# A fused attention and feed-forward kernel: the last attention block cut into one half and two quarters of its queries, one tanh moved to the end, two inverse deviations moved to GpSimd, new thresholds in the static schedule

## The chip, the cores and the metric

The kernel runs on one core of a Trainium2 chip. The metric is the device time of one execution in microseconds (us). The span, which the profile shows, starts with the first instruction and ends with the last; it is 1.8 to 2.1 us shorter than that time in most executions. Some executions show a stretch of half clock of TensorE, about 3.4 us long; they are called dipped below, and dipped and undipped ones are told apart throughout. Four of the fourteen profiles show such a dip; the other executions are sorted by their spans and mean clocks alone, so that for them it is a judgement.

The engines are named as in the profile: PE is TensorE, ACT is ScalarE, DVE is VectorE, POOL is GpSimd.

## The reference

```python
# x [1, 2048, 448] bf16; H = 16 heads of 28; F = 1792
xn = layernorm(x)
q, k, v = split_heads(xn @ wqkv)
p = softmax(q @ k.T / sqrt(28))
s = merge_heads(p @ v) @ wo
g = silu(gelu(xn @ w1 + b1) @ w2 + b2)
return x + s * g
```

## The kernel before

The scores are 16 blocks (4 groups of 4 heads, by 4 chunks of 512 queries), each of 64 tiles of 128 keys by 512 columns: 1024 tiles. PE writes score tiles into a ring of banks, ACT takes two or three tiles at a time through one exp instruction into the P buffers, PE multiplies P by the values. Some tiles are taken from ACT: DVE copies the scores out as integers ("eviction") and works out the exponential with four more operations and a scaling. Which tiles, is decided when the program is built: the code simulates its own schedule with a duration for each task, and a threshold for each block says how much backlog DVE may have (THS) and how near to the end of a block (SLACKS) a tile may still be taken.

```python
LATE_GAP, LATE_SUB = 3, 14
THS = (8.0, 4.0, 7.0, 6.0, 4.0, 6.0, 9.0, 6.0, 3.0, 3.0, 8.0, 8.0, 8.0, 3.0, 6.0, 8.0)
SLACKS = (6.0, 5.0, 6.5, 5.0, 9.0, 6.5, 9.0, 6.0, 3.0, 4.0, 6.0, 6.0, 8.0, 6.0, 8.0, 6.0)
SEM = 0.07                       # modelled handover between tasks
# ... cut: pick_late(u), whether unit u gives its last tile to DVE
        n = 64 if sub < NBLK - 1 else 16
        r = m % n
        if len(ms) < 3 or not K.late_on or sub == 0 or r < 4 or GU - 1 <= u <= GU + 1:
            return False
        left = (n - 1 - r) / 3.0 * 1.364 + SLACKS[m // 64]
        # ... cut: second tile of an open pair
            bl = K.backlog()
            one = max(bl, 4.1) + 7.2 > left
            if not K.ys or bl > THS[m // 64] or bl + 4.8 > left or sub > LATE_SUB:
                return False
```

The last block is worked as four quarters of 128 queries, so that little is left to do after the last exp; a score tile of a quarter holds four pieces of 128 columns.

```python
    def pieces(self, m):                        # block 15
        s, r = r // 16, r % 16
        return b, r % 4, [(4 * (r // 4) + k, 128 * s, 128, 128 * k) for k in range(4)], r == 15, s

    def p_epi4(self, s):                        # end of quarter s, cut to its operations
        # DVE tensor_copy(E, acc)                          cast
        # PE  matmul(bank, selb, E)                        sums of the four heads
        # DVE reciprocal(R, bank)
        # DVE tensor_tensor(dst, E, R, mult)               product
        # then: PE matmuls with wo (output), DVE multiply by the gate g, DVE add of x, DMA
```

The inverse deviation of the layernorm (rstd) of each chunk is a logarithm and an exponential on ACT, and the gate of each chunk is a tanh on ACT followed by four DVE operations:

```python
        yield _Task(ACT, lambda eng: eng.activation(K.lnv[:, sl], K.mv[:, sl, 1], ACTF.Ln, bias=K.epsc[:, 0:1]), ...)
        yield _Task(ACT, lambda eng: eng.activation(K.rstd[:, sl], K.lnv[:, sl], ACTF.Exp, scale=-0.5), ...)
        # ... cut
        yield _Task(ACT, lambda eng: eng.activation(sg, fb, ACTF.Tanh, scale=0.5), ...)     # 4 x 448 columns
```

The softmax here doesn't subtract the row's maximum and nothing guards it: scores larger than these inputs give would overflow.

## Time and profile before

| | before |
|---|---|
| time, three runs | 486.66 us (486.65 to 486.67) |
| span of the profiled execution | 484.67 us |
| first exp starts | 12.61 us |
| last exp ends | 478.45 us |
| tail after it | 6.22 us |
| busy: PE, ACT, DVE, POOL | 438.8, 471.8, 389.7, 34.5 us |
| tiles on DVE | 70 of 1024 |

I read such a kernel as three terms: the head up to the first exp, the stream of exps on ACT, and the tail. The prediction shows the lines for it. (Texts written earlier took tails from spans rounded to 0.1 us: 6.25 before. The figures here are worked out from unrounded times.) One more number is used below, the excess of waits. From the end of one exp to the end of the next, in long stretches without a wait, it is 1.343 us for three tiles and 0.917 us for two. What a step between two neighbouring exps takes beyond that is summed up as excess: 1.15 us for the kernel before.

### The profile page before, as it was taken

To read this page: it belongs to the slowest core of one execution; us is meant where nothing else is said; L and a number is where in the kernel's file an instruction comes from. 1 tells how busy PE (TensorE), PEld (TensorE's weight loads), DVE (VectorE), ACT (ScalarE), POOL (GpSimd) and SP (SyncE) were. 2 spreads that over 40 slices of the span, in tenths; PEclk is the share of its full clock that TensorE was granted. 3 is DMA by queue.
4 is the path that set the end of the run, shared out by engine and by line. 5 is a ranking of instruction groups with operands and counts; after the bars stand their busy time and mean duration, and the time that the engine had idled before them with its cause. 6 is when DMAs were issued, how large, how long until landed. Compare 5 with 4: busy or idle time off the path is not lost.

```text
span 484.7 us, 10440 instructions
## 1 busy us (share of the span) xinstructions
PE 438.8 (91%) x4393; PEld 170.2 (35%) x4428; DVE 389.7 (80%) x562; ACT 471.8 (97%) x393; POOL 34.5 (7%) x71
## 2 busy tenths in 40 slices
PE   6998989998899998899899989989999999989895
PEld 4443333332232323333323442233333333434553
DVE  8946789988769989979877968798887888878354
ACT  5999999999999999999999999999999999999994
POOL 7260000000001000000001000010100100010000
PEclk9999999999999999999999999999999999999998
DMA  8401000000000000000400000000010010201010
GB/s 252 143 8 29 1 0 1 1 2 3 0 1 1 1 1 1 1 3 0 134 1 0 1 2 0 1 2 8 31 39 1 2 39 1 64 13 41 1 62 20
DMA packets 8289, 11.11 MB, mean 23 GB/s; under 512 B 1649, under 2 KB 6897, under 8 KB 8242
## 3 DMA queue, kind: packets, MB, share of 16 engines
q1 hardware_dynamic: 8098, 10.21, 6.9%
q8 instruction: 35, 0.57, 0.5%
q10 hardware_dynamic: 144, 0.23, 0.1%
q14 instruction: 12, 0.10, 0.1%
HBM read 8.61 MB, written 1.84 MB: 22 GB/s over the span
## 4 chain that ended last, share of the span: by engine, by line
ACT 45%; PE 34%; issue 16%; DVE 3%; POOL 0%; ACTq 0%; DVEq 0%
ACT P L1136 43%; PE ring L1105 9%; PE acc L1322 5%; PE misc L1053 5%; PE ring L995 4%; PE acc L845 2%; PE misc L683 2%; PE misc L995 1%; PE misc L1411 1%; PE acc L827 1%; ACT h L1032 1%; ACT w L1067 1%; PE ring L937 1%; PE misc L1394 0%; PE misc L1246 0%
## 5 line engine op out<-in xcount | busy, mean ns | idle before, releaser
L1136 ACT ACTIVATE P<-ring 128x1536 bf16<-128x1536 f32 (+1 forms) x350 | 431.3, 1482 | 0.7 <-PE ring L1105 0.4
L1105 PE MATMUL ring<-qT,kT 32*128 32x512 bf16 (+1 forms) x1208 | 136.4, 349 | 29.7 <-ACT P L1136 23.5
L1322 PE MATMUL acc<-P,vaug 128*32 128x512 bf16 (+1 forms) x1146 | 94.8, 351 | 1.2 <-DVE E_sb L1372 0.5
L1105 PEld LDWEIGHTS ring<-qT,kT 32*128 32x128 bf16 x1208 | 36.6, 91 | 140.2 <-ACT P L1136 130.3
L1159 DVE TENSOR_SCALAR x_sb<-ring 128x512 int32<-128x512 f32 x62 | 42.6, 688 | 20.8 <-PE ring L1105 20.2
L1053 PE MATMUL misc<-w,h 128*128 128x448 bf16 x224 | 51.9, 355 | 0.1
L845 PE MATMUL acc<-ident,zero 128*128 128x128 bf16 x546 | 47.0, 221 | 0.6 <-DVE E_sb L1372 0.4
L1322 PEld LDWEIGHTS acc<-P,vaug 128*32 128x32 bf16 x1146 | 25.1, 94 | 49.9 <-issue 45.0
L845 PEld LDWEIGHTS acc<-ident,zero 128*128 128x128 bf16 x546 | 31.6, 98 | 20.7 <-issue 16.9
L995 PE MATMUL misc<-xnT,w 128*128 128x512 bf16 x125 | 35.2, 382 | 1.9 <-issue 1.4
L1384 POOL CAST rhi<-rc 128x16 bf16<-128x16 f32 x15 | 7.8, 521 | 403.7 <-DVE rc L1382 304.4
L978 DVE CAST h<-misc 128x512 bf16<-128x512 f32 x35 | 24.1, 687 | 9.8 <-PE misc L995 9.6
L1053 PEld LDWEIGHTS misc<-w,h 128*128 128x128 bf16 x224 | 17.5, 97 | 23.2 <-issue 11.3
L1276 DVE SCALAR_TENSOR_TENSOR kT<-kT 128x1024 f32<-128x1024 f32 (+1 forms) x20 | 23.3, 1167 | 0.3
L1278 DVE SCALAR_TENSOR_TENSOR kT<-kT 128x1024 f32<-128x1024 f32 (+1 forms) x20 | 23.3, 1167 | 0.3
L1280 DVE SCALAR_TENSOR_TENSOR x_sb<-x_sb,kT 128x1024 uint16<-128x1024 int32 (+1 forms) x20 | 23.3, 1164 | 0.4
L1274 DVE SCALAR_TENSOR_TENSOR kT<-kT 128x1024 f32<-128x1024 f32 (+1 forms) x20 | 23.3, 1163 | 0.4
L995 PE MATMUL ring<-xnT,w 128*128 128x512 bf16 x81 | 19.5, 380 | 0.9 <-ACT h L1032 0.7
L1274 DVE SCALAR_TENSOR_TENSOR w<-w 128x1024 f32<-128x1024 f32 (+1 forms) x17 | 19.7, 1159 | 0.3
L1278 DVE SCALAR_TENSOR_TENSOR w<-w 128x1024 f32<-128x1024 f32 (+1 forms) x17 | 19.7, 1157 | 0.3
L1280 DVE SCALAR_TENSOR_TENSOR x_sb<-x_sb,w 128x1024 uint16<-128x1024 int32 (+1 forms) x17 | 19.7, 1156 | 0.2
L1276 DVE SCALAR_TENSOR_TENSOR w<-w 128x1024 f32<-128x1024 f32 (+1 forms) x17 | 19.6, 1154 | 0.1
(142 smaller groups left out, 439.1 us busy)
## 6 DMA issues: line engine op xcount, KB each, us to landing
h<-in_A_x_dram SPq DMA_DIRECT2D x4, 448.0 KB, 3.3
w<-in_B_w_dram SPq DMA_DIRECT2D x1, 1568.0 KB, 7.3
x_sb<-in_A_x_dram SPq DMA_DIRECT2D x3, 448.0 KB, 5.5
w<-in_B_w_dram SPq DMA_DIRECT2D x1, 1344.0 KB, 8.2
out_dram<-h SPq DMA_DIRECT2D x6, 224.0 KB, 2.0
h<-in_A_wqkv_dram SPq DMA_DIRECT2D x3, 168.0 KB, 5.5
out_dram<-h SPq DMA_DIRECT2D x4, 112.0 KB, 1.7
wo<-in_A_wo_dram SPq DMA_DIRECT2D x16, 24.5 KB
```

Of the source, the lines that this page charges most:

```text
L845: ins = eng.matmul(K.acc[:, 0:128], K.zero[:, :], K.ident[:, :], start=False, stop=True, skip_group_check=True)
L978: yield _Task(DVE, lambda eng: eng.tensor_copy(dst, bank), [tok], wr, 0.69, 0.0, 2)
L995: ins = eng.matmul(bank, K.w1[:, kt, ft * 128:(ft + 1) * 128], K.xnT[:, kt, c * 512:(c + 1) * 512], start=(kt == 0), stop=(kt == KT - 1))
L1053: ins = eng.matmul(ps, hv[:, ft, t * 128:(t + 1) * 128], K.w2[:, ft, :], start=(ft == 0), stop=(ft == FT - 1))
L1105: return eng.matmul(K.ring[:, RB[m], col:col + nq], K.kT[32 * j:32 * j + 32, g, t * 128:(t + 1) * 128], K.qT[32 * j:32 * j + 32, g, c * 51 ...
L1136: return eng.activation(K.P[:, p0:p0 + n, :], K.ring[:, b0:b0 + n, :], ACTF.Exp, scale=SM_SCALE)
L1159: yield _Task(DVE, lambda eng, m=m, i=i, half=half: eng.tensor_scalar(K.ysb[i][:, 512 * half:512 * half + 512], K.ring[:, RB[m], :], SM_SC ...
L1274: yield _Task(DVE, lambda eng: eng.scalar_tensor_tensor(u, v, EXP_A, v, op0=ALU.add, op1=ALU.mult), [tv], [tu], d1, 0.0, 4)
L1276: yield _Task(DVE, lambda eng: eng.scalar_tensor_tensor(u, u, EXP_B, u, op0=ALU.add, op1=ALU.mult), [tu], [tu], d1, 0.0, 4)
L1278: yield _Task(DVE, lambda eng: eng.scalar_tensor_tensor(u, v, EXP_D, u, op0=ALU.mult, op1=ALU.add), [tv, tu], [tu], d1, 0.0, 4)
L1280: yield _Task(DVE, lambda eng: eng.scalar_tensor_tensor(pl.bitcast(dt.uint16), y, 2.0 ** -9, u, op0=ALU.mult, op1=ALU.add), ty + [tu], [K. ...
L1322: return eng.matmul(K.acc[32 * j:32 * j + 32, q0:q0 + nq], K.vaug[:, t, 4 * g + j, :], ap[:, col:col + nq], tile_position=(0, 32 * j), sta ...
```

## The change

Its intent is to take work out of the ACT stream: four small ACT instructions to GpSimd, a quarter of one tanh to the end, and more tiles to DVE, also in the last block, whose first half is now worked as one piece long enough to have such tiles. The half has 32 tiles of two pieces of 256 columns; two quarters follow. Repeated and mechanical parts are cut.

```diff
-LATE_GAP, LATE_SUB = 3, 14
-THS = (8.0, 4.0, 7.0, 6.0, 4.0, 6.0, 9.0, 6.0, 3.0, 3.0, 8.0, 8.0, 8.0, 3.0, 6.0, 8.0)
-SLACKS = (6.0, 5.0, 6.5, 5.0, 9.0, 6.5, 9.0, 6.0, 3.0, 4.0, 6.0, 6.0, 8.0, 6.0, 8.0, 6.0)
+LATE_GAP, LATE_SUB = 3, 15
+THS = (8.0, 4.0, 7.0, 8.0, 4.0, 7.0, 9.0, 6.0, 6.0, 8.0, 8.0, 8.0, 8.0, 8.0, 7.0, 3.0)
+SLACKS = (6.0, 5.0, 3.0, 5.0, 2.0, 6.5, 9.0, 6.5, 3.0, 4.0, 7.0, 6.0, 8.0, 6.0, 8.0, 3.0)
-SEM = 0.07
+SEM, OWN = 0.07, 0.03
@@ start_of
+        own = self.evsem[t.E]
-            s = max(s, b.tw + SEM)
+            s = max(s, b.tw + (OWN if b.w is not None and b.w[0] is own else SEM))
@@ p_ln2, chunks 2 and 3
+            yield _Task(POOL, lambda eng: eng.tensor_scalar(K.lnv[:, sl], K.mv[:, sl, 1], LN_EPS, None, op0=ALU.add), ...)
+            yield _Task(POOL, lambda eng: eng.tensor_tensor(K.rstd[:, sl], K.lnv[:, sl],
+                                                            K.mhalf[:, 0:1].to_broadcast([128, len(ts)]), ALU.pow), ...)
@@ p_silu, last chunk
-        yield _Task(ACT, lambda eng: eng.activation(sg, fb, ACTF.Tanh, scale=0.5), ...)
+        nt = 4 if c < C - 1 else 3
+        yield _Task(ACT, lambda eng: eng.activation(sg[:, 0:nt, :], fb[:, 0:nt, :], ACTF.Tanh, scale=0.5), ...)
+        if nt < 4:
+            yield ("until", lambda: K.exp_m == MTOT - 1)
+            # tanh of the fourth tile on ACT, then on POOL: o = tanh * fb; o = o + fb
@@ pieces, last block
-        s, r = r // 16, r % 16
-        return b, r % 4, [(4 * (r // 4) + k, 128 * s, 128, 128 * k) for k in range(4)], r == 15, s
+        if r < 32:
+            return b, r % 4, [(2 * (r // 4) + k, 0, 256, 256 * k) for k in range(2)], r == 31, 0
+        s, r = r // 16 - 1, r % 16
+        return b, r % 4, [(4 * (r // 4) + k, 128 * (s + 1), 128, 128 * k) for k in range(4)], r == 15, s
@@ pick_late
-        n = 64 if sub < NBLK - 1 else 16
+        n = 64 if sub < NBLK - 1 else 32
@@ p_epi4: ts = ((0, 1), (2,), (3,))[s]; one cast for the piece, then sums, reciprocal and product for each tile
```

## The prediction

> **What bounds the kernel now.** I read the page first: the busy totals, then the slices over time.
>
> ```profile
> PE 438.8 (91%) x4393; PEld 170.2 (35%) x4428; DVE 389.7 (80%) x562; ACT 471.8 (97%) x393; POOL 34.5 (7%) x71
> ...
> DVE  8946789988769989979877968798887888878354
> ACT  5999999999999999999999999999999999999994
> ```
>
> ScalarE (ACT) is full in every slice but the first and the last. VectorE (DVE) has holes, most of them in the last three slices (3, 5, 4 tenths). Next the busy time by stretches:
>
> ```profile
> core 0: us, PE busy (x) PEld busy (x) DVE busy (x) ACT busy (x) POOL busy (x), PEclk, DMA share, GB/s
> ...
> 233.00:260.00 27.00, 24.34 (x226) 8.29 (x229) 20.53 (x27) 27.00 (x23) 0.41 (x2) 1.00 0.19 59
> ...
> 287.00:314.00 27.00, 25.18 (x199) 8.75 (x198) 19.88 (x26) 26.97 (x22) 0.00 (x0) 1.00 0.01 2
> ...
> 435.00:449.00 14.00, 13.09 (x145) 6.06 (x143) 11.34 (x15) 14.00 (x12) 0.00 (x0) 1.00 0.10 35
> 449.00:462.00 13.00, 11.58 (x279) 6.35 (x277) 5.11 (x11) 13.00 (x11) 0.41 (x2) 1.00 0.06 19
> 462.00:478.50 16.50, 15.80 (x368) 9.38 (x365) 8.17 (x16) 16.45 (x13) 0.00 (x0) 1.00 0.12 38
> 478.50:484.70 6.20, 1.00 (x18) 0.45 (x18) 2.56 (x5) 0.00 (x0) 0.00 (x0) 0.80 0.06 21
> ```
>
> ACT is busy 27.0 of 27.0 us in stretch after stretch; it stops at about 478.5. So the span is three terms: a head to the first exp (12.6 us in the timeline), an ACT stream without gaps from 12.6 to 478.45 (465.85 us), and a tail of 6.25 us with no ACT work. Anything taken out of the stream shortens the kernel by its own length, unless it makes ACT wait. DVE works only 5.1 of 13 us from 449 to 462, where the last block starts: that is the hole the change aims at.
>
> What one ACT step costs comes from the groups by form:
>
> ```profile
> L1136 ACT ACTIVATE P<-ring 128x1536 bf16<-128x1536 f32 x255 | 356.7, 1615 | 0.0
> L1136 ACT ACTIVATE P<-ring 128x1024 bf16<-128x1024 f32 x94 | 101.9, 1126 | 0.7 <-PE ring L1105 0.4
> ```
>
> The durations overlap from one instruction to the next, so they are not steps. Steps come from start to start: the score matmuls that follow each three-tile exp start at 461.89 and, eleven steps on, at 476.67, so 1.344 us a step. Two-tile steps: seven exps in a row from 18.94, the last ending at 25.48, so starting 1.1 before; (24.4 - 18.94)/6 = 0.91 us. One tile of 512 columns moved from ACT to DVE is worth 1.344 - 0.91 = 0.43 us. Today 70 tiles of 1024 are on DVE: 62 evictions of ring tiles plus 8 around the gelu stage. The 94 two-tile exps agree: 32 at the start, 62 robbed of a tile. No eviction starts after 434.9, because the last block is forbidden to have any.
>
> **What the Trainium skill says.** "Perfetto Trace Analysis", section Identifying the Most-Contended Engine, says to take occupancy for ScalarE and work on that engine first; with 97% the trace agrees. "ScalarE: Activation LUTs", section What ACT_TABLE_LOAD costs, gives 0.833 ns per element in a lane and some 93 ns of overlap between neighbours: 512 columns would be 0.427 us, and the 0.43 from the steps agrees. The section on table sets of that page puts tanh in the exp set, so moving a tanh behind the exps should cost no table load; the three loads in the trace (1.283 us each) are at the start and around gelu, none at the tanhs. "GPSIMD Engine Reference", section Elementwise, gives about 2.6 cycles per element for an operation with two inputs (0.97 us for 448 elements at its 1.2 GHz, an estimate from that page). The trace has one of this size, the 128x448 square at 1.033 us, and I use that.
>
> **The change, part by part.**
>
> 1. Rstd of chunks 2 and 3. Removed from ACT: two logarithm-and-exponential pairs. At 18.48 the logarithm starts and at 18.94 the next big exp: 0.46 us. The second pair runs from 25.33 to 25.81: 0.48. Sum 0.94 us out of the stream. Added on GpSimd: an add and a power on four columns. A four-column operation there took 0.229 us; the power is in no trace, and the 1.1 us that the code's own schedule gives it is all I have. So rstd comes about 0.23 + 1.1 + 0.2 of handovers = 1.5 us after the statistics (17.89), at 19.4 instead of 19.03. That is 0.4 us later, while ACT comes to use the keys 0.5 to 0.9 earlier. This matters for chunk 2: its keys are written from 26.95 to 27.69, and the scores of the seventeenth two-tile unit start at 27.93, so they follow almost at once. The ring of scores gives ACT only some 0.3 us of reserve there. Of the 0.94 us I therefore expect 0.55 to stay (estimate: sometimes the delay is absorbed, since the transposes of that chunk start 1.5 us after their inputs; sometimes all but 0.3 is lost to a wait for keys).
>
> 2. The last tanh. One tanh on 1792 columns takes 408.92 to 410.51 on ACT, 1.59 us of stream. With 1344 columns it should be 1.59 - 448 x 0.833 ns = 1.22. Saved: 0.37 us. The fourth part runs behind the last exp, where ACT is idle. It then needs two GpSimd operations: 0.47 (tanh) + 2 x 1.03 + 3 handovers of 0.07 = 2.74 us after the last exp. The tail today takes from 478.45 to 481.48, 3.03 us, before the multiply by this gate: last matmuls, copy 0.29, sum matmul, reciprocal 0.96, product 0.29, output matmul. So it fits with about 0.3 us to spare, and the tail stays at 6.25, or grows by a few tenths if GpSimd is slowed by VectorE beside it. One VectorE operation of 0.62 us falls away as well.
>
> 3. The last block as a half and two quarters. Keys and queries are the same; score tiles of the half are two pieces of 256 columns, not four of 128, so PE gets fewer instructions, and the last quarter, which sets the tail, is untouched. What counts is that the half may use VectorE exps. It has 32 tiles, about 32/3 x 1.344 = 14.3 us of ACT. A pair of tiles on VectorE is two evictions of 0.69, one scaling of 0.69 and four operations of 1.22: 6.95 us. VectorE has 7.9 us free from 449 to 462. One pair fits, perhaps a pair and a single: 2 to 4 tiles, I take 3. Saved: 3 x 0.43 = 1.3 us. The end of the half waits for these exps, but two quarters of 7.2 us each follow in which that can be made up, and the P buffers (21 tiles, seven units) cover 9 us.
>
> 4. The new thresholds and the own-engine handover of 0.03. They change no instruction's cost, only how many tiles the static schedule gives to VectorE and in which order. VectorE is idle 6.5 us in 233 to 260 and 7.1 in 287 to 314; just there the thresholds go up most (3 to 6, 3 to 8), also later (3 to 8), while two early blocks get a stricter end. Over the fourteen stretches of 27 us from 44 to 422 the idle time is about 57 us. If 11 of it become exps at 3.5 us a tile, that is 3 tiles, 1.3 us. This number is a choice: I can see the room but not what the schedule does with it. From -1 to +8 tiles is possible.
>
> Sum: 0.55 + 0.37 + 1.3 + 1.3 = 3.5 us. 486.66 - 3.5 = 483.1.
>
> **The rivals.**
>
> A. VectorE becomes the bound. It is at 80% over the span, 25.1 of 27 in the fullest stretches. If the higher thresholds overfill it, evictions release their ring tiles late, the scores wait and then ACT. Against it: the same rule already bounds the backlog, and ACT shows no such wait today. It would leave the gain at 0.5 to 1.5 us: 485 to 486.
>
> B. The keys of chunk 2 come late and ACT waits about 1 us near 27 us. For it: the tight timing of step 1. Against it: the slack ahead of the transposes. It would cost 0.4 more than my sum: 483.5.
>
> C. The GpSimd products end after the output matmul, and the tail grows by 0.3 to 0.8 us: at worst 483.9.
>
> D. The re-tuning fills VectorE's idle time better than I think, with ten more tiles in all than I count: 4 us more, 479. For it: 57 us of idle. Against it: much of it is pieces under 2 us between operations that wait for PE.
>
> **Range and chances.** A, B and C together could take about 2 us from the gain, D could add 2 or 3 in the plausible case. So 480.5 to 485.3 for 8 in 10. Faster by over 2% means below 476.9, which needs 9.7 us, or some 19 more tiles on VectorE beside the rest (66 us of its time); 2% chance. Slower by over 2% would need a new stall of 10 us: 1%. The rest is within 2%.
>
> **What would show it.** Right: ACT still without gaps from 13 to the end of its exps; no logarithm at 18 or 25 us; one tanh of 1344 columns, one of 448 after the last exp; about 76 VectorE tiles (two to four of them after 445 us); a tail of 6.2 us from the last exp. Wrong in step 1: an ACT wait on PE near 27 us, or a power far from 1.1 us. Wrong in step 2: the last multiply waits for GpSimd, not PE. Wrong in 3 or 4: a tile count outside 71 to 80, or new ACT waits at block ends. The most doubtful term is 4.

## More of the kernel before

The tail of the kernel before, from its timeline (start us, duration us, engine, line, operation, output and input):

```profile
478.60 0.41 PE L1322 MATMUL acc<-P,vaug 128*32 128x128 bf16 x16 [0.35 <-ACT P L1136]
479.05 0.29 DVE L1354 CAST E_sb<-acc 128x128 bf16<-128x128 f32 x1 [2.71 <-PE acc L1322]
...
479.40 0.23 PE L1357 MATMUL ring<-E_sb,selb 128*128 128x128 bf16 x1 [0.40 <-DVE E_sb L1354]
479.67 0.96 DVE L1360 RECIPROCAL w<-ring 128x128 f32<-128x128 f32 x1 [0.32 <-PE ring L1357]
```

The attention matmuls start 0.15 us after the last exp, the sum matmul 0.35 us after the start of the cast. The chain is free of other work.

## The result, and the profile after

| | before | changed |
|---|---|---|
| median of six executions | 486.75 us (486.65 to 487.69) | 483.99 us (483.74 to 485.26) |
| undipped executions | | 483.74 to 483.99 (four) |
| dipped executions | | 484.90 and 485.26 (two) |
| ratio of means | | 0.9945 (0.9931 to 0.9959) |

A ratio here is the mean time of one kernel's runs over that of the other's in the same rounds, so it is not quite the ratio of the medians. The class "within 2%" was right, and 483.99 lies in the range, 0.9 above the predicted 483.1. The gain of medians is 2.8 us, where 3.5 was forecast. The output is correct.

The changed kernel's page, the lines that stand against those of before:

```profile
PE 438.5 (91%) x4232; PEld 168.1 (35%) x4268; DVE 407.6 (84%) x592; ACT 468.8 (97%) x390; POOL 43.2 (9%) x77
...
DVE  8946888989978989989878749899997999889785
ACT  5999999999999999999999999999999999999994
```

ACT lost 3.0 us of busy time, DVE gained 17.9, and ACT is still full. The stretches at the end, by busy time of each engine:

```profile
core 0: us, PE busy (x) PEld busy (x) DVE busy (x) ACT busy (x) POOL busy (x), PEclk, DMA share, GB/s
...
449.00:462.00 13.00, 12.11 (x220) 6.21 (x218) 10.26 (x19) 13.00 (x11) 0.95 (x2) 1.00 0.01 3
462.00:476.50 14.50, 13.70 (x300) 8.10 (x300) 9.99 (x19) 14.50 (x13) 0.00 (x0) 1.00 0.12 42
476.50:483.10 6.60, 1.89 (x24) 0.73 (x22) 3.86 (x8) 0.42 (x1) 2.06 (x2) 0.77 0.16 52
```

DVE now works 10.26 of 13 us from 449 to 462 (5.11 before): the hole was used. The last stretch is 6.6 us long, not 6.2. The groups by form on ACT (the mean is in ns, after the busy time):

```profile
L1160 ACT ACTIVATE P<-ring 128x1536 bf16<-128x1536 f32 x249 | 349.3, 1606 | 1.0 <-PE ring L1129 1.0
L1160 ACT ACTIVATE P<-ring 128x1024 bf16<-128x1024 f32 x100 | 108.2, 1133 | 0.7 <-PE ring L1129 0.6
...
L1080 ACT ACTIVATE w<-w 128x1344 bf16<-128x1344 bf16 x1 | 1.4, 1423 | 0.0
```

255 three-tile exps became 249 and 94 two-tile ones became 100: six tiles more are on DVE, 76 in all, and one tanh has 1344 columns. On GpSimd the power is there, two of them:

```profile
L645 POOL TENSOR_TENSOR rstd<-lnv,mhalf 128x4 f32<-128x4 f32 x2 | 2.1, 1035 | 0.2
```

**The dip.** The profiled execution was a dipped one (484.90). By stretches of the length of the dip:

```profile
39.80:43.20 3.40, 3.07 (x35) 1.16 (x31) 2.27 (x6) 3.40 (x4) 0.00 (x0) 1.00 0.17 38
43.20:46.60 3.40, 3.36 (x14) 0.59 (x14) 1.38 (x2) 2.65 (x3) 0.00 (x0) 0.50 0.00 0
46.60:50.00 3.40, 3.02 (x29) 1.06 (x27) 2.62 (x6) 3.16 (x3) 0.02 (x1) 1.00 0.00 0
```

and the second of these stretches in an undipped execution of the same kernel (the next run):

```profile
43.20:46.60 3.40, 3.13 (x22) 1.00 (x23) 2.20 (x5) 3.40 (x4) 0.00 (x0) 1.00 0.00 0
```

For 3.4 us the granted clock is 0.50, PE executes 14 matmuls where the undipped execution has 22, and ACT has work for only 2.65 us of 3.40. The Trainium skill, page "TensorE: Matmul & The Clock Gate", section "Part 1: The HAM clock gate (the "warmup" mystery)", says that the clock is either half or full, and judged over a free-running window of about 3.4 us; this trace agrees, with 0.50 and 3.4 us. The kernel before with new thresholds alone, profiled below, shows the same dip, from 44.1 to 47.5 us, and before itself has executions with spans of 485.6 to 486.3 us beside those of 484.7 to 485.4. So a dip is no effect of the change, and I compare undipped executions from here on. What sets it off stays open.

### The profile page after: what moved, and what is told of

The parts are those of the page before. It is cut to its first block, busy times and chain, and to the rows that moved or that the text cites. A ratio compares the mean times of both kernels' runs of the same rounds, so it can differ in the third digit from the quotient of the medians.

```text
span 483.1 us, 10155 instructions
## 1 busy us (share of the span) xinstructions
PE 438.5 (91%) x4232; PEld 168.1 (35%) x4268; DVE 407.6 (84%) x592; ACT 468.8 (97%) x390; POOL 43.2 (9%) x77
## 4 chain that ended last, share of the span: by engine, by line
ACT 45%; PE 32%; issue 17%; DVE 5%; ACTq 0%; DVEq 0%
ACT P L1160 42%; PE ring L1129 9%; PE acc L1346 6%; PE misc L1065 4%; PE acc L857 3%; PE misc L695 2%; ACT h L1044 2%; PE misc L1007 1%; PE acc L839 1%; PE misc L949 1%; PE misc L1442 1%; PE ring L1007 1%; ACT w L1080 1%; PE ring L949 1%; DVE kT L1298 0%
## 5 line engine op out<-in xcount | busy, mean ns | idle before, releaser
L1129 PE MATMUL ring<-qT,kT 32*128 32x512 bf16 (+2 forms) x1144 | 136.5, 360 | 26.1 <-ACT P L1160 22.0
L1346 PE MATMUL acc<-P,vaug 128*32 128x512 bf16 (+2 forms) x1074 | 95.0, 363 | 1.0 <-issue 0.5
L1183 DVE TENSOR_SCALAR x_sb<-ring 128x512 int32<-128x512 f32 x68 | 46.8, 688 | 14.2 <-PE ring L1129 13.0
L1415 POOL CAST rhi<-rc 128x16 bf16<-128x16 f32 x15 | 10.3, 686 | 402.5 <-DVE rc L1413 255.6
L857 PE MATMUL acc<-ident,zero 128*128 128x128 bf16 x516 | 44.8, 221 | 0.0
L857 PEld LDWEIGHTS acc<-ident,zero 128*128 128x128 bf16 x516 | 29.8, 98 | 21.3 <-issue 19.4
L1304 DVE SCALAR_TENSOR_TENSOR x_sb<-x_sb,kT 128x1024 uint16<-128x1024 int32 (+1 forms) x24 | 26.7, 1111 | 0.5
L1302 DVE SCALAR_TENSOR_TENSOR kT<-kT 128x1024 f32<-128x1024 f32 (+1 forms) x24 | 26.6, 1110 | 0.5
L1298 DVE SCALAR_TENSOR_TENSOR kT<-kT 128x1024 f32<-128x1024 f32 (+1 forms) x24 | 26.5, 1104 | 0.6
L1300 DVE SCALAR_TENSOR_TENSOR kT<-kT 128x1024 f32<-128x1024 f32 (+1 forms) x24 | 26.4, 1102 | 0.2
L1298 DVE SCALAR_TENSOR_TENSOR w<-w 128x1024 f32<-128x1024 f32 (+1 forms) x18 | 20.3, 1128 | 0.3
L1300 DVE SCALAR_TENSOR_TENSOR w<-w 128x1024 f32<-128x1024 f32 (+1 forms) x18 | 20.3, 1130 | 0.2
L1302 DVE SCALAR_TENSOR_TENSOR w<-w 128x1024 f32<-128x1024 f32 (+1 forms) x18 | 20.3, 1129 | 0.1
```

The costliest lines, as they stand in the source:

```text
L857: ins = eng.matmul(K.acc[:, 0:128], K.zero[:, :], K.ident[:, :], start=False, stop=True, skip_group_check=True)
L1129: return eng.matmul(K.ring[:, RB[m], col:col + nq], K.kT[32 * j:32 * j + 32, g, t * 128:(t + 1) * 128], K.qT[32 * j:32 * j + 32, g, c * 51 ...
L1183: yield _Task(DVE, lambda eng, m=m, i=i, half=half: eng.tensor_scalar(K.ysb[i][:, 512 * half:512 * half + 512], K.ring[:, RB[m], :], SM_SC ...
L1298: yield _Task(DVE, lambda eng: eng.scalar_tensor_tensor(u, v, EXP_A, v, op0=ALU.add, op1=ALU.mult), [tv], [tu], d1, 0.0, 4)
L1300: yield _Task(DVE, lambda eng: eng.scalar_tensor_tensor(u, u, EXP_B, u, op0=ALU.add, op1=ALU.mult), [tu], [tu], d1, 0.0, 4)
L1302: yield _Task(DVE, lambda eng: eng.scalar_tensor_tensor(u, v, EXP_D, u, op0=ALU.mult, op1=ALU.add), [tv, tu], [tu], d1, 0.0, 4)
```

## The experiments

**The changed kernel again.** No edit: the same kernel. Its five executions were all undipped.

> The changed kernel, unaltered. Two levels are expected, because the six first runs had two: about 483.9 us where the granted TensorE clock is 1.0 over the whole span, about 485.0 where it is 0.993 (the profiled run had the clock at 0.50 from 44 to 46 us and ACT waiting 0.96 us for scores at 46.84). Theory: the dip alone is the 1.2 us between the levels, and a trace without it has ACT waits of only 0.6 us after the first exp. Rival: the levels are something else, and a trace at clock 1.0 still shows that wait.

Measured: 483.73 us (483.72 to 483.90), before 486.67 to 487.34 undipped; ratio 0.9922 (0.9908 to 0.9937). The span is 481.93. Its waits of ACT for score tiles, with total, number and longest, first in the dipped profile and then here:

```profile
ACT P L1160 <- PE ring L1129: 1.5, 3, 1.0
```

```profile
ACT P L1160 <- PE ring L1129: 0.5, 2, 0.3
```

The dip cost 1.15 us of span (483.08 against 481.93), 1.0 of it in that one wait. With the dip gone, the balance between the two profiled executions can be made, all in us. "Other ACT work" is the length by which it widens the step between two exps.

| term | before | changed | difference |
|---|---|---|---|
| start of the first exp | 12.61 | 13.20 | +0.59 |
| six tiles at 0.426 | | | -2.56 |
| rstd of chunks 2 and 3 (2 x 0.41) | 0.82 | 0 | -0.82 |
| rstd of chunk 1, now ahead of the first exp | 0.41 | 0 | -0.41 |
| last tanh | 1.58 | 1.20 | -0.38 |
| excess of waits | 1.15 | 1.62 | +0.47 |
| stream (sum of the last five, 0.02 unexplained) | 465.84 | 462.12 | -3.72 |
| tail | 6.22 | 6.61 | +0.39 |
| span | 484.67 | 481.93 | -2.74 |

The stream lost 3.72 us, but 0.41 of that is the pair of chunk 1, which the prediction did not have and which only stands in the head now; without it the stream lost 3.31 of the predicted 3.5. Head and tail gave back 0.57 beside that pair. The longer tail and the terms of the stream are what the next runs take apart.

A profile's head has some chance in it. The matmuls of the first transposes start 107 ns apart until the trace's first record of a full clock, and 55 ns apart from there on. That record lies anywhere between 6.3 and 9.7 us in the fourteen profiles: at 7.76 before, 8.66 here. The first input statistics also start 0.16 us later here than before (3.87 against 3.71).

**Pinned tiles.** A change in one part moves the static schedule, and with it which tiles go to DVE. For some runs I therefore gave `pick_late` a list of tiles in place of its thresholds. With the changed kernel's own list it builds the changed kernel's program again (checked by building both: they differ in line numbers alone).

```diff
+PIN = [(m, h, m == p[-1]) for p in PAIRS for h, m in enumerate(p)]
@@ pick_late
-            if not K.ys or bl > THS[m // 64] or bl + 4.8 > left or sub > LATE_SUB:
+        if not PIN or PIN[0][0] > m ...:
```

**The two tiles of the half given back to ACT.** The list without tiles 974 and 980. Theory: each is worth 0.43, and the DVE exps of the half also disturb the tail. Rival: the tail has another cause.

> The changed kernel with the two VectorE tiles of the last block's half given back to ACT; all other 74 tiles fixed as in the changed kernel. Theory: ACT pays 2 x 0.43 = 0.86 us more, but the half ends without waiting for VectorE's chain (465.2 us now), so the third output of the last chunk is out before the last exp and the tail falls from 6.65 back to about 6.25: net +0.4 to +0.5, about 484.4. Rival: the tail's extra 0.4 has another cause (the moved gate, the single free bank), it stays, and the kernel is +0.86: 484.8.

Measured: 484.60 to 484.67 us undipped (two dipped, 486.08 and 486.09); ratio 0.9950 (0.9934 to 0.9965). The stream is 462.97, so 0.85 longer, which is 2 x 0.426; excess 1.62 as in the changed kernel. The tail is 6.61, as there: it did not recover. The half is worth its two tiles and no more, and the longer tail does not come from DVE exps in it; here the rival held.

**All six tiles given back.** The list of the kernel before, 70 tiles, on the changed kernel.

> The changed kernel with exactly the 70 VectorE tiles of the kernel before. Theory: every tile is worth 0.43 us of ACT, six are 2.6 us, less 0.4 that the tail gains back: +2.2, about 486.1. Rival: the four tiles outside the last block were won only by overfilling VectorE, part of them comes back as waits, and their loss costs less than 0.25 us each: 484.9 to 485.3.

Measured: 486.96 to 486.99 undipped (two dipped, 487.61); ratio 0.9993 (0.9979 to 1.0007). The stream is 465.49: 2.52 longer than with 74 tiles. Four tiles are 1.70 of it; the other 0.80 is excess (2.42 against 1.62). That list was made for another schedule, which may be why; this run does not show it. Without its six tiles the changed kernel is level with before, so the rest of the change brings about as much as its longer tail and this misfit cost; a clean value of the tiles cannot be read from it.

**Rstd back on ACT, tiles pinned.**

```diff
@@ p_ln2
-        if c < 2:
+        if c < 4:
```

> The changed kernel with rstd of chunks 2 and 3 on ACT again, the same number of VectorE tiles in each block. Theory: the two pairs cost ACT 0.94 us, less the 0.30 us wait at 28.3 us that the changed kernel has there: +0.6, about 484.5. Rival 1: the late keys ate the whole gain: 483.9, no difference. Rival 2: the wait at 28.3 has nothing to do with rstd: +0.94, 484.8.

Measured: 488.41 us (488.38 to 488.73); ratio 1.0019 (1.0006 to 1.0032). That is 4.7 us more than the changed kernel. The waits of ACT show why this run measures something else:

```profile
ACT P L1162 <- PE acc L1339: 2.6, 2, 1.7
```

ACT waits 2.6 us for P buffers (the attention matmuls that release them), at two places around 403 and 405 us; the changed kernel waits for no P buffer. The likely reason, not tested, is that the pinned tiles don't fit the schedule that comes of the shifted start. As a whole the run is confounded, but not at its beginning: the first 32 exps are block 0, which gives no tile to DVE in any of these kernels. From the start of the first exp to the end of the 32nd, less the 0.41 of chunk 1's pair where it lies inside, the traces give:

| first 32 exps | us |
|---|---|
| before | 30.85 |
| changed | 30.35 |
| changed, rstd back on ACT (this run) | 31.23 |
| before, rstd on GpSimd alone (next run) | 30.85 |
| changed, own-engine handover of 0.07 (below) | 30.85 |

So in the changed order rstd on GpSimd is worth 0.88 us here, and the change as a whole 0.50.

**Rstd on GpSimd alone, in the kernel before.** Only `p_ln2` as in the change; 70 tiles, the same as before. Theory: of the 0.8 to 0.9 us some half stays. Rival: the keys come late and eat it.

> The kernel before with rstd of chunks 2 and 3 on GpSimd alone; the schedule keeps the same 70 tiles in each block. Theory: two pairs of 0.47 us leave ACT, and ACT waits some 0.3 us more near 28 us: -0.6 us against the kernel before. Rival 1: late keys eat all of it: 0. Rival 2: no wait at all: -0.94.

Measured: 486.73 to 487.06 undipped (one dipped, 487.73), before 486.58 to 487.09 undipped; ratio 0.9996 (0.9982 to 1.0009). The stream is 465.84, to the hundredth that of before: 0.82 of ACT work is gone and 0.82 of excess has come (1.97 against 1.15). The rival held. Around chunk 2 in this run, from the timelines of GpSimd, PE and ACT: the power, the key matmuls (L692), the scores of the next unit (L1114) and the exp that waits for them:

```profile
18.88 1.04 POOL L642 TENSOR_TENSOR rstd<-lnv,mhalf 128x4 f32<-128x4 f32 x1
```

```profile
26.72 0.38 PE L692 MATMUL ring<-xnT,wk 128*128 128x512 bf16 x1 [0.16 <-DVE h L654]
...
28.82 0.45 PE L1114 MATMUL ring<-qT,kT 32*128 32x512 bf16 x4
```

```profile
29.25 1.94 ACT L1145 ACTIVATE P<-ring 128x1024 bf16<-128x1024 f32 x2 [0.42 <-PE ring L1114]
```

Rstd is ready at 19.92, where before had it at 19.03. The keys' matmuls start at 26.72 (26.09 before), the key write at 28.02 (26.95 before), the scores of the next unit at 28.82, and ACT waits. The first exp of this profile is 0.59 later too (13.20), so that much of each of these delays ACT does not feel. What is left is the chain that the prediction described as rival B: it takes all that rstd had freed, in the first 32 exps already (30.85 in both).

**The changed kernel without the own-engine handover of 0.03.**

```diff
-SEM, OWN = 0.07, 0.03
+SEM, OWN = 0.07, 0.07
```

> The changed kernel with the own-engine handover of the schedule back at 0.07 (the schedule then finds the same 76 tiles, six of them two or three places later or earlier). Theory: only the order changes; at the start VectorE writes the first queries 0.4 us earlier (11.64 instead of 12.04) and the first exp starts at about 12.6 instead of 13.2, but a logarithm and exponential of 0.33 us then stand inside the stream: -0.25 us, 483.5. Rival: the schedule's worse idea of VectorE's time costs more waits later, and it is 484 or more.

Measured: 484.86 and 485.01 undipped, four dipped (485.74 to 486.10); ratio 0.9966 (0.9953 to 0.9980). As in the changed kernel, 76 tiles are on DVE (six of them two or three places off), so this constant, which describes no work at all, is worth about 1.2 us. It only changes the order in which the built schedule puts tasks. The first exp starts at 13.20, not at the expected 12.6, but that expectation was not tested: the clock was full only from 9.49 us in this execution, and the sixteen first transposes, here and before, took

```profile
8.30 1.60 PE L770 MATMUL ring<-ident,h 128*128 128x128 bf16 x16
```

```profile
8.09 1.22 PE L758 MATMUL ring<-ident,h 128*128 128x128 bf16 x16
```

So up to 0.4 of the 1.2 us may be this execution's. The stream is 0.56 longer: 0.41 is the pair of chunk 1, which stands behind the first exp again, and 0.13 is excess (1.75). In the first 32 exps the loss is 0.50, a part of which comes back later, where steps that the changed kernel loses time at (0.36 near 315 us) are missing here. The key write of chunk 2 is at 28.01 again, as with rstd alone, where the changed kernel has it at 26.70; and the excess has the same two steps as the run with rstd alone, 0.41 and 0.53 (0.40 and 0.53 there), ending at 22.4 and 30.3 us in both. And the tail is 7.33, for the multiply and add of the third tile (from 479.06) are put ahead of the multiply of the last (480.02). So the rstd part pays only in the new order, which brings chunk 2's keys forward:

```profile
25.62 1.04 PE L695 MATMUL ring<-xnT,wk 128*128 128x512 bf16 x4
26.59 0.39 PE L1129 MATMUL ring<-qT,kT 32*128 32x512 bf16 x2
26.91 1.07 PE L949 MATMUL ring<-wv,xnT 128*128 128x128 bf16 x16
27.91 0.58 PE L1129 MATMUL ring<-qT,kT 32*128 32x512 bf16 x4
```

In these lines of the changed kernel (undipped) the key matmuls begin 1.1 us earlier than in the run with rstd alone. What delays the scores at 27.91 here are, by the order of the lines, no longer keys (written from 26.70 to 27.45) but sixteen value matmuls (L949) put ahead of them, and ACT waits 0.30 us at 28.34.

**The whole tanh in its old place, gates on DVE, tiles pinned.**

```diff
-        nt = 4 if c < C - 1 else 3
+        nt = 4
@@ t_oev
-                    [tok, K.b_g3 if (c, t) == (C - 1, 3) else K.b_g[c]], ...
+                    [tok, K.b_g[c]], ...
```

> The changed kernel with the last chunk's tanh whole again and all four gates on VectorE; the same 76 tiles. Theory: ACT's stream grows by 1.59 - 1.22 = 0.37 us, the tail (6.58 us in the changed kernel at clock 1.0, 6.25 before) stays, as the second GpSimd product ends 0.7 us before it is needed: +0.37, about 484.1. Rival: the moved gate is what lengthened the tail; then the tail goes back to 6.25 and the sum is nil: 483.75.

Measured: 484.11 to 484.14 us in four executions, 485.39 and 485.64 in two. The spans of those two are 482.4 and 482.1, about as short as the others' (482.1 to 482.3): their extra time lies outside the span. Ratio 0.9945 (0.9930 to 0.9960). The stream is 462.49, the 0.37 expected, and the tail 6.62 beside 6.61. So moving the tanh is worth its 0.37, and neither the late tanh nor the two GpSimd products lengthen the tail.

**The tail: banks given back earlier.** In the changed kernel's tail (undipped run) the chain is crowded:

```profile
474.88 0.74 PE L1442 MATMUL ring<-wo,qT 128*128 128x448 bf16 x3
...
475.56 0.41 PE L1346 MATMUL acc<-P,vaug 128*32 128x128 bf16 x16
...
475.89 0.93 PE L1442 MATMUL ring<-wo,qT 128*128 128x448 bf16 x4
476.02 0.29 DVE L1377 CAST E_sb<-acc 128x128 bf16<-128x128 f32 x1 [0.27 <-PE acc L1346]
...
476.66 0.22 PE L1388 MATMUL ring<-E_sb,selb 128*128 128x128 bf16 x1
...
476.96 1.03 POOL L1097 TENSOR_TENSOR h<-h,w 128x448 bf16<-128x448 bf16 x1
...
478.73 0.62 DVE L1451 TENSOR_TENSOR h<-ring,h 128x448 bf16<-128x448 f32 x1 [0.16 <-PE ring L1442]
```

The attention matmuls start 0.24 us after the last exp (475.32), behind three output matmuls, where it was 0.15; and four output matmuls of the third tile stand between the cast and the sum matmul, 0.64 us apart where it was 0.35. Together that is 0.38 us, of the 0.39 by which the tail is longer. The last multiply waits for PE, and the second product had ended 0.74 us before it. The third tile's output comes so late, I thought, because the two tiles of the half share one free bank. So the edit frees banks of the ring one unit earlier:

```diff
@@ p_exps
+            if u == NU - 3:
+                for k in range(len(UNITS[NU - 1]), n):
+                    K.banks.append((K.ring[:, b0 + k, :], K.b_ring[b0 + k]))
```

> The changed kernel, with the two banks of the score ring that the last unit (one tile) does not use given back one unit earlier. Theory: the tail grew because the third output of the last chunk found one free bank only, so its four output matmuls (0.93 us) stand between the last attention matmul and the sum matmul; with banks earlier they go before the last exp: the tail falls by 0.3, 483.4. Rival: the last outputs wait for something else and the tail stays at 6.58: 483.75.

Measured: 483.85 to 484.04 us in four executions, 484.56 in one; ratio 0.9931 (0.9917 to 0.9945). No gain: the tail is 6.73. (The profiled execution is the one of 484.56; it has a dip at 291 us, far from the tail.)

```profile
476.38 0.62 DVE L1454 TENSOR_TENSOR h<-ring,h 128x448 bf16<-128x448 f32 x1
...
476.56 1.03 POOL L1095 TENSOR_TENSOR h<-w 128x448 bf16<-128x448 bf16 x1 [21.45 <-ACT w L1093]
476.91 0.28 DVE L1380 CAST E_sb<-acc 128x128 bf16<-128x128 f32 x1
477.11 0.73 DVE L1456 TENSOR_TENSOR h<-h 128x448 bf16<-128x448 bf16 x1
```

The matmuls did move ahead, and their place in the chain was taken by DVE: the third tile's multiply now runs before the cast, and its add before the reciprocal, 0.73 us long in place of 0.39. The Trainium skill, page "SBUF — State Buffer", section "SBUF: two separate sides", says that a VectorE operation with two inputs in this memory and a GpSimd operation that reads this memory exclude each other: the one that starts second waits. The 0.73 beside a GpSimd product that runs from 476.56 to 477.59 agrees in kind. Earlier banks shift the third tile's work from one engine to another; they do not take it out of the chain.

**Four quarters again.** The changed kernel with `pieces` and the end of a quarter as before, tiles pinned to 74.

> The changed kernel with the last block in four quarters again and without the two VectorE tiles there (the other 74 fixed); so it differs from the run t74 (484.67 us, tail 6.63) only in half against two quarters. Theory: the half hands over two outputs at once to the one free bank, and that crowding is what lengthened the tail; with quarters the tail is back at 6.25 and the time is 484.3. Rival: the tail has grown for another reason (the moved tanh has been ruled out, 6.57 without it); it stays above 6.5, and the time is 484.65.

Measured: 484.31 to 484.59 us in five executions, 486.18 dipped; ratio 0.9942 (0.9927 to 0.9957). Beside the half with 74 tiles (484.60 to 484.67, on another chip, where before had an undipped median of 487.08 against 486.71 here) this is no clear difference. The profile fell in a dipped execution; of its tail:

```profile
478.43 0.29 DVE L1368 CAST E_sb<-acc 128x128 bf16<-128x128 f32 x1 [0.36 <-PE acc L1337]
478.78 0.23 PE L1379 MATMUL ring<-E_sb,selb 128*128 128x128 bf16 x1 [0.40 <-DVE E_sb L1368]
...
480.11 0.44 DVE L1385 TENSOR_TENSOR qT<-E_sb,w 128x128 bf16<-128x128 bf16 x1
...
480.60 0.55 PE L1433 MATMUL ring<-wo,qT 128*128 128x448 bf16 x1 [1.60 <-DVE qT L1385]
```

From cast to sum matmul it is 0.35 us again, so those 0.29 us of the crowding do come with the half. The attention matmuls, though, still start 0.24 us after the last exp (477.73), so the other 0.09 does not. And the tail is 6.66 all the same. The last matmul takes 0.55 us (0.36 elsewhere): the granted clock is 0.50 from 480.59 on, so that this 0.19 belongs to this execution. The product takes 0.44 (0.29) while a GpSimd product of the moved gate runs, from 479.37 to 480.40. Without these three terms (0.09, 0.19 and 0.15) the tail would be 6.23, an estimate from the numbers above; whether the 0.15 comes in every execution, only an undipped profile could tell.

**The thresholds alone.** The kernel before with the new THS and SLACKS; it gets 74 tiles.

> The kernel before with the new thresholds alone: the schedule then picks 74 tiles, one more in each of four blocks. Theory: 4 x 0.426 = 1.70 us less ACT and no new wait: 1.7 under the kernel before. Rival: with the old order the fuller VectorE releases score tiles late, waits take back a third or more: 1.1 or less.

Measured: 485.72 to 485.83 us in five executions (one dipped, 487.19), before 486.47 to 486.97 undipped; ratio 0.9975 (0.9959 to 0.9991). That is 0.9 of the 1.70 that four tiles are worth: something took nearly half. The profile fell in the dipped execution, but in the changed kernel the same dip altered the excess between 32 and 60 us alone (1.64 against 0.43). Outside that stretch the excess is 1.14 (0.68 before): 0.46 more, with one step of 0.69 behind this wait for scores:

```profile
434.38 2.79 ACT L1136 ACTIVATE P<-ring 128x1536 bf16<-128x1536 f32 x2 [0.58 <-PE ring L1105]
```

The rest is the head (0.22 later, as are the inputs by 0.18) and the tail (0.21 longer; the last matmul, at half clock from 480.99 us on, takes 0.55 and not 0.36), and may be this execution's alone. So waits took about a quarter of the four tiles' worth, somewhat less than the rival said.

**More tiles still.** Two new sets of thresholds for the changed kernel, found by asking the built schedule how many tiles it can place: both give 79. No other edit.

```diff
-THS = (8.0, 4.0, 7.0, 8.0, 4.0, 7.0, 9.0, 6.0, 6.0, 8.0, 8.0, 8.0, 8.0, 8.0, 7.0, 3.0)
-SLACKS = (6.0, 5.0, 3.0, 5.0, 2.0, 6.5, 9.0, 6.5, 3.0, 4.0, 7.0, 6.0, 8.0, 6.0, 8.0, 3.0)
+THS = (8.0, 6.0, 10.0, 10.0, 4.0, 7.0, 8.0, 6.0, 6.5, 10.0, 7.0, 10.0, 7.0, 7.0, 9.0, 5.0)
+SLACKS = (6.0, 3.0, 5.0, 8.0, 7.0, 7.0, 10.0, 6.0, 9.0, 6.0, 8.0, 8.0, 11.0, 4.0, 7.0, 4.0)
```

> The changed kernel with other thresholds and slacks alone: its schedule now gives 79 of the 1024 tiles to VectorE in place of 76, everything else of the change as it is. Theory (the stream is bound by ScalarE, a tile is worth 0.426 us where no wait comes in its place): 3 x 0.426 = 1.28 us shorter stream, 482.5 us in undipped executions (482.2 to 482.9), 0.991 of the kernel before or less. Rival (VectorE is full by now and the waits for the ring and for P take back what more tiles give, as they took part of it with the thresholds alone): 483.4 to 484.2 us, the same as the change, with the excess of ScalarE's waits up by 1 us or more from 1.62 us.

> As the other, with a second set of thresholds that also gives 79 tiles, put in other places of the blocks. Theory: 482.2 to 482.9 us, the two sets within 0.4 us of each other, since only the number of tiles counts. Rival: 483.4 to 484.2 us, or the two sets over 0.6 us apart, since the place of each tile decides what waits it brings.

Measured, first set: 482.05, 482.26 and 482.27 us undipped, three dipped (483.64 to 483.77); ratio 0.9913 (0.9896 to 0.9930). Its stream is 460.68, 1.44 shorter than the changed kernel's: 1.28 for three tiles, and the excess fell to 1.45. The only wait for score tiles that its profile lists:

```profile
ACT P L1160 <- PE ring L1129: 0.3, 1, 0.3
```

Second set: 482.66 to 483.17 us in four executions, two of them at a slightly lower mean clock (0.995 and 0.994), and 484.06 in one; ratio 0.9913 (0.9899 to 0.9928). Its stream is 461.10: 1.28 for the tiles, less 0.25 of more excess, with two steps of 0.36 and 0.29 near 316 us that the first set lacks. So DVE was not full at 76 tiles, and the value of a tile held. The place of the tiles decides some tenths beside it. By stream and by undipped times the first set beats both kernels; over before it gains 4.6 us undipped (482.26 against 486.85, medians of the undipped executions). The ratios, which take in its three dipped executions, do not part it from the changed kernel (0.9896 to 0.9930 and 0.9908 to 0.9937).

## Why the prediction was right

Its number was right by its own mechanism, with some luck in the terms: two errors of one tile cancelled each other. Against its sum of 3.5 us stand, from the undipped profiles: tiles 2.56 (2.6 expected), tanh 0.38 (0.37), rstd 0.82 less the 0.47 of new excess (0.55), and, not in the sum, the tail's 0.39 and the head's 0.18 to be taken off. That is 2.72, and 2.74 by the spans.

1. **What bounds the kernel** held. Each thing taken off ACT shortened the stream by its own length, in every run where no wait came in its place: tiles by 0.426 each, from 79 down to 74; the tanh by 0.37.
2. **Rstd** was to bring 0.55 of 0.94. The step is smaller, 0.82, since it is taken from end to end of the exps and not from the start of the logarithm. The power takes 1.035 us, near the 1.1 assumed. Alone the part brings nothing, as the late keys take all 0.82 back; in the changed order 0.50 stays over the first 32 exps. The prediction's "0.55 to stay" was a mean of two cases, so that its closeness is partly luck: which case came was decided by a part, the handover constant, that it counted as worth nothing apart from tiles.
3. **The tanh** was to bring 0.37 and brought 0.38. That it "fits with about 0.3 us to spare" was cautious: 0.74 us. No multiply waits for GpSimd.
4. **The half** was to bring three tiles, and got two, 0.85 us. "The last quarter, which sets the tail, is untouched" is the step that failed: its instructions are the same, but the tail is 0.39 longer. The trace shows output matmuls of the third tile in the chain of the last, 0.38 in all. That neither the gate nor the DVE exps make the tail of the changed kernel longer, two runs show; that banks cure it, one run refuted; with four quarters 0.29 of the crowding is gone, but other terms lengthen the tail there, so that no run has brought it back to 6.22 with the rest of the change in place. The prediction had put a longer tail down to GpSimd, and in the changed kernel that was wrong.
5. **The thresholds** were to bring three tiles and brought four. With the half's two that is the 76 predicted. The prediction called this size a choice; that three and three became four and two is luck for the sum. By themselves the thresholds gave only 0.9 us for four tiles.
6. **The head** was not in the sum. It is 0.59 later, of which 0.41 is counted as the moved pair. How much is the kernel's is not shown: the input statistics start 0.16 later in this execution and the clock becomes full 0.90 later. With rstd alone and with the old handover the first exp starts at 13.20 too, with the pair still behind it, in executions whose clock was full only at about 9.5 us; with the thresholds alone, where the head's instructions are those of before, it starts at 12.83, with inputs 0.18 later.

Of the rivals, A (DVE full) was refuted by the runs with 79 tiles; B happened in full with rstd alone; C gave the right size for the wrong reason; D was not reached by the change, but three tiles more, the 79, brought 1.44 us of stream.

## What to carry to other kernels

When one engine is full, price a change by the step from the end of one instruction to the end of the next, count how many steps it removes, and then look for the wait that may take their place. In a static schedule a part has no value of its own: the order that the rest gives it decided here between 0 and 0.5 us for the first 32 exps. Hold the distribution of work fixed only if the schedule around it stays the same too; otherwise the experiment measures the misfit. And look for a stretch that the distribution cannot touch, as block 0 here: it can be read even in a confounded run.

## What the Trainium skill lacked or had wrong

- "GPSIMD Engine Reference", section 3.1: it has no power. Here a power of 128x4 values takes 1.035 us, where adding a constant to as many values takes 0.228.
- "TensorE: Matmul & The Clock Gate", Part 1: its table puts half clock down to at least one idle window of about 3.4 us, and a later section, on cycling through PSUM queues, tells of a clock that swings when PE often idles briefly between groups of matmuls, without a figure for how much. Here the clock fell to half for 3.4 us, once in an execution, after a stretch in which PE was busy 3.07 of 3.40 us (ends of matmuls are modelled); an execution of the same kernel with 3.13 of 3.40 there did not dip. By spans and mean clocks it befell about a third of the executions here, before and after; the one that was profiled in the changed kernel was 1.15 us longer.
